# Decode attention over a 2048-key window plus a bilinear GLU: TensorE's unrolled program becomes a loop of seven turns over five heads, and four engines' programs are wrapped in a loop of two turns

## The chip, the core and the metric

The kernel runs on one core of one Trainium2 chip. The metric is the device time of one execution in microseconds (us). The kernel before takes 376.09 us, the median of three runs (375.97, 376.09 and 376.46).

## What is computed

Two tokens, one for each of the batches (B = 2), with D = 512 features, go through a layer norm, and the normalised token `xn` feeds two branches whose sum is added to the token. All data are float32.

```python
W = min(4096, max(256, Sk // 4))                  # 2048 of the 8192 cached keys
q = (xn @ wq)                                     # 32 heads of 128
scores = einsum("bhqd,bhkd->bhqk", q, k[:, :, Sk - W:]) * 128 ** -0.5
o = einsum("bhqk,bhkd->bhqd", softmax(scores), v[:, :, Sk - W:])
out = x + o @ wo + ((xn @ w_gate) * (xn @ w_up)) @ w_down    # inner width 1376
```

Every head has its own keys and values, so each of the 159.47 MB of caches and weights is used once.

## The kernel before

**The stream.** `blocks()` lists what is read, in order, as fields of some words for each of the 128 partitions: `k` and `v` (4096 words for each head, both batches side by side), `wq`, `wo`, and the weights of the GLU (`wg`, `wu`, `wr`, `wd`). The host lays the fields out in that order in one array, `stream`. SyncE's queue (SP) carries it into three slots of SBUF, `step0` to `step2`, in turn; a transfer into a slot starts when the last field that stands in it has been used (`done`, `pump`). Most transfers fill a slot with 7936 KB: the keys of one or two heads and pieces of the values of heads some three back. Behind the last full slots come shorter transfers: the last keys, the last three heads' values, and rows of `w_down`, down to 256 KB.

**One head** passes through these steps:
- `project_q`, TensorE: the token, copied over 128 columns (`xnb`), times `wq`, so that q stands in PSUM once on each partition, for both batches; four heads share a bank pair (`q0`, `q1`).
- `products`, VectorE: keys times q, in place in the slot, reading q from PSUM. `sums`, VectorE: the sum over the 128 features, which gives the scores `s` (128 x 32). `maxima`: VectorE takes each partition's largest (`m`), GpSimd the largest over partitions (`mm`).
- `weights`, ScalarE: minus the scaled maximum (`nm`), the exponentials into `p`, their sums `rs`; GpSimd sums these over partitions (`sum`), VectorE inverts (`rec`, in `reciprocals`, called behind the next head's maxima).
- `weigh`, TensorE: eight chunks of the values with `p` as stationary operand, summed in the PSUM bank `o_ps`. `copy_out`, ScalarE: the bank to `o_sb`. `transpose`, TensorE, into the bank `tr`; ScalarE scales by `rec` into `oT`. `project_o`, TensorE: `oT` times `wo`, added up in the bank `acc`.

The heads' values go through `weigh` in groups of two and one; the last heads alone.

**Order.** `Flow` records every operation as it is written in Python, finds what each depends on, and `emit` writes each engine's program in that order, one instruction behind the other with no branch. So an engine that waits holds up everything written behind it. A semaphore wait is set where an operation needs another engine or a transfer. All recorded instructions carry the line of `emit` (L243), so the profile is read by the names of the tiles.

**The end.** Behind the last keys the order is written by hand: the last heads' `pv`, `transpose` and `project_o` one by one, with matmuls into a spare bank between them (`keep_busy`) that compute nothing. The last head's values come before the last rows of `w_down`; `accumulate` spreads the final products over four partition groups of `acc`.

Of the kernel before, what the change touches and what calls it, by code (L numbers as in the profile page):

```python
# [8 lines left out]
ALU = mybir.AluOpType  # L9
# [8 lines left out]
J = W // P  # L18
# [6 lines left out]
LAG = 3  # L25
RB = 8
# [4 lines left out]
HG = 4  # L31
GC = HG * DH
JG = J // 4
CK, CQ, CO = B * J * DH, NC * GC, D
CP = CQ // NC
UNIT = CK + max(CP, CO)
STEP = 31 * FB
NP = 6
NV = CK // FB
KS = [3, 1, 2, 1, 2, 2, 1, 2, 2, 2, 1, 2, 2, 2, 1, 2, 2, 1]  # L40
WD = [(0, 2), (2, 4), (4, 7), (7, NFC - 1), (NFC - 1, NFC)]
NS = 3
BUFS = 3
BASE = 30 * 1024
FX = FR // NS

# [10 lines left out]
def blocks():  # L57

    def wd(n):
        return [("wd", i, D) for i in range(*WD[n])]

    def k(h):
        return [("k", h, CK)] + ([("wq", h, CP)] if h + HG < H else [])  # L70

    def v(h):
        return [("v", h, CK), ("wo", h, CO)]

    def gu(half):
        n = NC * (FH[half][1] - FH[half][0])
        return [("wg", half, n), ("wu", half, n)]

    ones = [("pick", 0, 8 * B), ("rows", 0, NFB * B)]
    first = [("x", 0, B * NC)] + ones + [("w", 0, NC * DH)]  # L80
    ahead = [[("w", 1, CQ - NC * DH)], gu(0) + gu(1), [("wr", 0, NS * P)] + wd(0)]
    pieces = [(h, n) for h in range(H - 1 - LAG) for n in range(NV + 1)]
    loads, h = [], 0
    for i, n in enumerate(KS):
        fields = (ahead[i] if i < len(ahead) else []) + sum((k(h + j) for j in range(n)), [])
        h += n
        room = (STEP - sum(w for _, _, w in fields)) // FB if i > 1 else 0
        taken, pieces = pieces[:room], pieces[room:]
        for g in sorted({g for g, _ in taken}):
            assert g < h - n  # L90
            ns = [m for t, m in taken if t == g]
            parts = [m for m in ns if m < NV]
            if parts:
                p0, p1 = parts[0], parts[-1] + 1
                fields.append(("vp", (g, p0, p1), FB * (p1 - p0)))
            if ns[-1] == NV:
                fields.append(("wo", g, CO))
        assert not pieces or pieces[0][0] >= h - NP
        loads.append(fields)
    assert not pieces and h == H - 1  # L100
    loads += [k(H - 1) + v(H - 1 - LAG) + wd(1)]
    out = [(("f", 0), first)] + [(("s", i), fields) for i, fields in enumerate(loads)]
    late, last = ("s", len(loads)), ("s", len(loads) + 1)
    out += [(late, v(H - 3)), (late, v(H - 2)), (last, [("v", H - 1, CK)])]
    out += [(last, [("wo", H - 1, CO)] + wd(2))]
    return out + [(last, wd(n)) for n in range(3, len(WD))]


class Flow:
# [7 lines left out]
    def __init__(self, nc):  # L117
        self.nc = nc
        self.units = {
            "pe": nc.tensor, "dve": nc.vector, "act": nc.scalar, "pl": nc.gpsimd, "sp": nc.sync,  # L120
        }
        self.ops, self.seen, self.free = [], {}, {}
        self.low = -(-nc.sbuf_base // 32) * 32
# [38 lines left out]
    def add(self, unit, make, writes, reads):  # L162
        n = len(self.ops)
        deps = set()
        for aps, write in ((reads, False), (writes, True)):
            for ap in aps:
                if not isinstance(ap.tensor, (bass.SBTensorHandle, bass.PSumTensorHandle)):
                    continue
                name, p0, p1, f0, f1 = self.box(ap)
                kept = []  # L170
                for old in self.seen.get(name, []):
                    m, w, a0, a1, b0, b1 = old
                    if m != n and (write or w) and a0 < p1 and p0 < a1 and b0 < f1 and f0 < b1:
                        deps.add((m, w))
                        if write and p0 <= a0 and a1 <= p1 and f0 <= b0 and b1 <= f1:
                            continue
                    kept.append(old)
                self.seen[name] = kept + [(n, write, p0, p1, f0, f1)]
        self.ops.append((unit, make, deps))
# [3 lines left out]

    def emit(self):
        nc, ops = self.nc, self.ops
        place, count = [], {}
        for n, (unit, make, deps) in enumerate(ops):
            key = ("dma", n) if make[0] == "dma_start" else unit
            count[key] = count.get(key, 0) + 1
            place.append((key, count[key]))  # L190
        knows = [None] * len(ops)
        known = {unit: {} for unit in self.units}
        waits = []
        for n, (unit, make, deps) in enumerate(ops):
            have = known[unit]
            need = {}
            for m, wrote in deps:
                key, at = place[m]
                if key == unit and (unit == "pe" or unit in ("dve", "act") and not wrote):
                    continue  # L200
# [7 lines left out]
            ]  # L208
            for m in keep:
# [11 lines left out]
        told = {m for keep in waits for m in keep} | {len(ops) - 1}  # L221
        sems, value, at = {}, {}, {}
        order = sorted({place[m][0] for m in told}, key=lambda key: (key in ("dve", place[-1][0]), str(key)))
        if order[-1] != place[-1][0]:
            order.append(order.pop(-2))
        for key in order:
            sems[key] = nc.alloc_semaphore("done_" + (key if isinstance(key, str) else f"load{key[1]}"))
# [7 lines left out]
        for n, (unit, (method, args, kwargs), _) in enumerate(ops):  # L235
            eng = self.units[unit]
            keep = sorted(
                waits[n], key=lambda m: (isinstance(place[m][0], tuple) and m >= landed, m)
            )
            landed = max([landed] + [m for m in keep if isinstance(place[m][0], tuple)])  # L240
# [8 lines left out]
            if n == len(ops) - 2:  # L249
                assert unit == "dve"  # L250
                nc.vector.sem_clear(range(nums[0], nums[-2]))
        assert unit == "sp"
# [19 lines left out]
def sliding_attention_plus_glu_kernel(  # L272
# [13 lines left out]
    ]  # L286


    todo, at = [], 0
    for key, fields in blocks():  # L290
        todo.append((key, fields, at))
        at += P * pitch(fields)
    tiles, used, left, got = {}, {}, {}, {}
    for key, fields, _ in todo:
        left[key] = left.get(key, 0) + len(fields)

    def pump():
        while todo:
            key, fields, at = todo[0]
            if key not in tiles:  # L300
                if key[0] == "f":
                    n = sum(w for _, _, w in fields)
                    tiles[key] = flow.tile([P, n], "first")
                elif not slots:
                    return
                else:
                    tiles[key] = slots.pop(0)
                used[key] = 0
            todo.pop(0)
            c0 = used[key]  # L310
            for kind, i, w in fields:
                got[kind, i] = (tiles[key][:, used[key] : used[key] + w], key)
                used[key] += w
            c1 = used[key]
            src = stream[at : at + P * pitch(fields)].rearrange("(p i) -> p i", p=P)
            sp.dma_start(tiles[key][:, c0:c1], src[:, : c1 - c0])

    def done(kind, i):
        _, key = got.pop((kind, i))
        left[key] -= 1  # L320
# [501 lines left out]
```

## Time and profile before

| what | value |
|---|---|
| median of the three runs | 376.09 us |
| the profiled execution's span | 374.6 us; the median is 1.5 us more, which lies around the span |
| DMA, mean | 426 GB/s, 3950 packets, 159.70 MB |
| TensorE matmul / weight load | 248.4 us (66%) / 86.8 us (23%), 1094 each |
| VectorE | 295.1 us (79%), 147 instructions |
| ScalarE | 58.1 us (16%), 259 |
| GpSimd | 25.3 us (7%), 78 |

The span runs from the first instruction to the last. "Busy" is time inside instructions; a share of the whole span mixes the stream's long middle with its start and its end, so the stages are read apart: landings of transfers from the chain of waits, durations of single operations from the timeline, the granted clock of TensorE (1.00 is full speed) from stretches of a few us. In a row of the timeline the first number is the start, the second the time, x16 the count of instructions merged into the row, and the bracket the idle time before them and what ended it. A float32 matmul of the program stands as two MATMUL records in the trace, so x16 is eight of the program's.

### The profile page before, as it was taken

The numbers are of one execution on the slowest core, as the hardware profiler recorded it, in microseconds if no ns is written. First come the engines' busy times: TensorE is split into PE (matmuls) and PEld (weight loads), VectorE is DVE, ScalarE is ACT, GpSimd is POOL, SyncE is SP. The second block draws the span as 40 slices with busy tenths as digits, with TensorE's granted clock in tenths as the row PEclk, the third lists the DMA queues.
The fourth block names the chain that finished last, engine by engine and source line by source line (L and its number), as shares of the span: only waits on it lengthen the run. The fifth ranks groups of instructions, "written<-read, shape, count | busy, mean of one in ns | idle before, by whom it ended". The sixth has DMA issues, their size and how long they took to land.

```text
span 374.6 us, 2741 instructions
## 1 busy us (share of the span) xinstructions
PE 248.4 (66%) x1094; PEld 86.8 (23%) x1094; DVE 295.1 (79%) x147; ACT 58.1 (16%) x259; POOL 25.3 (7%) x78
## 2 busy tenths in 40 slices
PE   3167675896578157855658585781488647476997
PEld 3033124231132013211212121320122112111344
DVE  3069998994599994599999945999999459999760
ACT  1002012111022012110202020300121201111232
POOL 1000000100001000000000000010001000000010
PEclk9759695898689758896969886998689868666999
DMA  8999999999999999999999999999999999999996
GB/s 345 420 465 454 450 432 435 434 434 424 427 427 434 434 434 434 436 434 441 434 435 429 434 434 434 434 429 434 434 435 434 429 434 434 428 426 416 414 432 250
DMA packets 3950, 159.70 MB, mean 426 GB/s; under 512 B 466, under 2 KB 610, under 8 KB 994
## 3 DMA queue, kind: packets, MB, share of 16 engines
q1 hardware_dynamic: 3938, 159.54, 98.6%
q8 instruction: 8, 0.13, 0.1%
q14 instruction: 4, 0.03, 0.0%
HBM read 159.47 MB, written 0.07 MB: 426 GB/s over the span
## 4 chain that ended last, share of the span: by engine, by line
DMA 64%; DVE 26%; PE 7%; ACT 1%; issue 0%; SPq 0%
DMA step<-in_stream_dram 64%; DVE s L243 13%; DVE step L243 13%; PE q L243 3%; PE acc L243 2%; PE o_ps L243 2%; PE tr L243 1%; ACT o_sb L243 0%; DVE m L243 0%; ACT oT L243 0%; DVE rec L243 0%; SPq L243 0%; DVE o_out L243 0%
## 5 line engine op out<-in xcount | busy, mean ns | idle before, releaser
L243 DVE TENSOR_TENSOR step<-step,q 128x4096 f32<-128x4096 f32 x31 | 136.8, 4411 | 47.0 <-DMA step<-in_stream_dram 47.0
L243 DVE TENSOR_REDUCE s<-step 128x32 f32<-128x4096 f32 x32 | 141.4, 4419 | 1.1
L243 PE MATMUL q<-step,xnb 128*128 128x512 f32 (+1 forms) x128 | 79.0, 759 | 80.5 <-DMA step<-in_stream_dram 80.5
L243 PE MATMUL o_ps<-step,p 128*16 128x512 f32 (+1 forms) x512 | 98.5, 730 | 11.2 <-DMA step<-in_stream_dram 11.2
L243 PEld LDWEIGHTS q<-step,xnb 128*128 128x128 f32 x128 | 28.0, 238 | 123.5 <-DMA step<-in_stream_dram 92.9
L243 PE MATMUL acc<-step,oT 128*9 128x512 f32 (+1 forms) x88 | 39.1, 604 | 8.7 <-ACT oT L243 8.7
L243 PE MATMUL tr<-first,o_sb 128*128 128x2 f32 (+2 forms) x198 | 29.1, 266 | 17.9 <-ACT o_sb L243 12.0
L243 PEld LDWEIGHTS tr<-first,o_sb 128*128 128x128 f32 x198 | 26.8, 205 | 40.6 <-ACT o_sb L243 31.3
L243 PEld LDWEIGHTS o_ps<-step,p 128*16 128x16 f32 x512 | 17.6, 107 | 78.6 <-issue 64.9
L243 ACT COPY o_sb<-o_ps 128x512 f32<-128x512 f32 (+1 forms) x24 | 13.8, 576 | 121.4 <-PE o_ps L243 121.4
L243 POOL PARTITION_ALL_REDUCE mm<-m x32 | 11.3, 355 | 268.6 <-DVE m L243 258.7
L243 ACT ACTIVATE nm<-mm 128x2 f32<-128x2 f32 x32 | 6.5, 203 | 148.0 <-POOL mm L243 148.0
L243 ACT ACTIVATE p<-s,nm 128x16 f32<-128x16 f32 x64 | 19.2, 300 | 1.0
L243 POOL PARTITION_ALL_REDUCE sum<-rs x32 | 12.7, 398 | 69.1 <-ACT p L243 69.1
L243 ACT ACTIVATE oT<-tr,rec 128x1 f32<-128x1 f32 x64 | 12.2, 260 | 27.0 <-PE tr L243 27.0
L243 DVE TENSOR_TENSOR step<-step,tr 128x4096 f32<-128x4096 f32 x1 | 4.4, 4422 | 14.8 <-DMA step<-in_stream_dram 14.8
L243 ACT ACTIVATION_READ_ACCUMULATOR p<-s,nm 128x1 f32 x64 | 11.9, 187 | 0.0
L243 PE MATMUL o_ps<-step,xn 128*2 128x512 f32 (+1 forms) x48 | 10.1, 548 | 0.0
L243 PEld LDWEIGHTS acc<-step,oT 128*9 128x9 f32 x88 | 4.6, 94 | 21.1 <-ACT oT L243 14.5
L243 DVE TENSOR_TENSOR o_out<-acc,x_nat 128x128 f32<-128x128 f32 x1 | 0.3, 292 | 8.4 <-PE acc L243 8.4
L243 DVE TENSOR_REDUCE m<-s 128x2 f32<-128x32 f32 x32 | 6.0, 186 | 1.1
L243 DVE RECIPROCAL rec<-sum 128x2 f32<-128x2 f32 x32 | 5.0, 155 | 1.9 <-POOL sum L243 1.9
(43 smaller groups left out, 41.5 us busy)
## 6 DMA issues: line engine op xcount, KB each, us to landing
step<-in_stream_dram SPq DMA_DIRECT2D x14, 7936.0 KB, 37.7
step<-in_stream_dram SPq DMA_DIRECT2D x2, 7680.0 KB, 32.0
step<-in_stream_dram SPq DMA_DIRECT2D x1, 7872.0 KB, 58.2
step<-in_stream_dram SPq DMA_DIRECT2D x1, 7808.0 KB, 38.8
step<-in_stream_dram SPq DMA_DIRECT2D x1, 4864.0 KB, 30.3
step<-in_stream_dram SPq DMA_DIRECT2D x2, 2304.0 KB, 19.6
step<-in_stream_dram SPq DMA_DIRECT2D x1, 2048.0 KB, 18.3
step<-in_stream_dram SPq DMA_DIRECT2D x1, 1024.0 KB, 19.8
```

Source lines behind the costliest of these rows:

```text
L243: made = getattr(eng, method)(*args, **kwargs)
```

## The change

**Layout.** Batch 0 lies on partitions 0 to 63 and batch 1 on 64 to 127 (`PB` = 64), for keys, values and q alike. A head still has 4096 words of keys and of values on each partition. q needs one matmul for both batches, and the maxima and the exponentials are written for each half of the partitions.

**The stream.** Three heads' keys come ahead (`AHEAD` = 3). Then six turns (`T` = 6) of three full slots of 7680 KB each bring the keys of five heads (`G` = 5), the values of the five heads three back, and the next turn's `wq`. In turn t the slot `step0` holds two heads' keys, the values of one head and five chunks of the next; `step1` holds two heads' keys, the rest of that head, a further one and one chunk; `step2` holds `wq`, one head's keys, and the rest of the values. The last turn has no fifth head of keys, and the last values and rows of `w_down` follow in eight shorter transfers. One row of `w_down` (`HOLE`) fills the gap in the last `wq`.

**TensorE's program.** The parts `q`, `a` and `b` of a turn (`part_q`, `part_a`, and `part_b` with `part_c`) read and write the same addresses in every turn, so they are written once, in a hardware loop of seven turns; the seventh does `part_a` alone. In the loop TensorE can't wait for growing semaphore values: at each waiting place it waits for a token of the engine concerned (`done_tokensp`, `done_tokenact`) and takes one away. For a transfer, SP itself waits for the landing and then gives the tokens (`tell`), in the order of its queue. `q` is in one PSUM tile of 640 columns, and ScalarE copies it to SBUF (`q_sb`, two buffers by turns, the second in the tile `first`), from where `products` reads it.

**The wrapping.** TensorE's, ScalarE's, VectorE's and GpSimd's programs each stand in a loop of two turns with `hint_back_edge`; in the first turn a branch skips all of it. SP's doesn't.

**The end.** The matmuls of `keep_busy` are gone. The last two heads' values go through one bank together; the last head is not split in two column halves any more.

```diff
+PB = P // B
+J = W // PB
+G = 5
+T = (H - 2) // G
+AHEAD = H + 1 - G * T
+SPLIT = [[0, 1], [2, 3, 4]]
+VA, VB = 5, 1
+STEP = 30 * FB
...
+        with self.nc.Fori(0, 2, engines=(eng.engine,), hint_back_edge=True) as turn:
+            with eng.If(turn > 0):
+                yield
...
+            if method == "tell":
+                m = args[0]
+                eng.wait_ge(sems[place[m][0]], value[m]).then_inc(sems["token", unit], tokens[n])
+                return
...
+                for key in sorted(points[part[0], part[2]]):
+                    eng.wait_ge(sems["token", key], 1).then_inc(sems["token", key], -1)
...
+            with nc.tensor.Fori(0, max(turns.values())) as turn:
+                for section, ns in body.items():
+                    short = turns[section] < max(turns.values())
+                    with nc.tensor.If(turn < turns[section]) if short else contextlib.nullcontext():
+                        for n in ns:
+                            write(n)
...
+    def project_q(t):
+        w = got["wq", t].rearrange("p (c n) -> p c n", c=NC)
+        for c in range(NC):
+            for n in range(0, GC, FB):
+                n1 = min(n + FB, GC)
+                pe.matmul(
+                    q_ps[:, n:n1], xnb[:, c, :], w[:, c, n:n1],
+                    start=(c == 0), stop=(c == NC - 1),
+                )
+        if t < T - 1:
+            done("wq", t)
+        act.copy(q_sb[t % 2], q_ps[:, :GC])
...
+    def scores(h, then=None):
+        products(h)
+        sums(h)
+        if then:
+            then()
+        maxima(h)
+        weights(h)
+        if h >= 1:
+            reciprocals(h - 1)
...
+    def part_a(t):
+        with flow.loop("a", t):
+            weigh(G * t, 0, NV)
+            weigh(G * t + 1, 0, VA)
+    def post(t, group):
+        d = transpose(group, copy_out(group))
+        scale_out(group, d)
+        for n in SPLIT[group]:
+            project_o(G * t + n)
+    def part_b(t):
+        with flow.loop("b", t):
+            weigh(G * t + 1, VA, NV)
+            post(t, 0)
+            weigh(G * t + 2, 0, NV)
+            weigh(G * t + 3, 0, VB)
+    def part_c(t):
+        with flow.loop("b", t):
+            weigh(G * t + 3, VB, NV)
+            weigh(G * t + 4, 0, NV)
+            post(t, 1)
+    for t in range(T):
+        part_q(t)
+        h = AHEAD + G * t
+        scores(h, lambda: part_a(t))
+        scores(h + 1)
+        scores(h + 2, lambda: part_b(t))
+        scores(h + 3)
+        if h + 4 < H:
+            scores(h + 4, lambda: part_c(t))
+        else:
+            reciprocals(h + 3)
+            part_c(t)
+    part_a(T)
+    down(HOLE)
+    acc_sb = flow.tile([M, D], "acc_sb")
+    dve.tensor_copy(acc_sb, acc)
+    weigh(H - 1, VA, NV)
+    o_sb = copy_out(0)
...
+    for c in chunks[:3]:
+        down(c)
     project_o(H - 2)
-
-    o_sb = flow.ring([P, 4 * DH], "o_sb", 2)
...
     project_o(H - 1)
-    down(3)
-    down(4)
+    for c in chunks[3:]:
+        down(c)
```

**Where instructions move.** At the end of ScalarE's program before, the exponentials of the last two heads (head 30 writes `p0`, head 31 `p1`) stand between the copies of single groups (`o_sb`); heads 25 to 28 are copied ahead of both:

```order
L243 COPY o_sb0_116<-o_ps0 128x512
L243 ACTIVATE oT1_64<-tr,rec1_111 128x1 x2
L243 ACTIVATE oT2_65<-tr,rec2_112 128x1 x2
L243 ACTIVATE oT3_66<-tr,rec3_113 128x1 x2
L243 COPY o_sb1_117<-o_ps1 128x512
L243 ACTIVATE oT0_63<-tr,rec4_114 128x1 x2
L243 ACTIVATE nm0_92<-mm0_86 128x2
L243 ACTIVATE p0_57,rs0_98<-s0_74,nm0_92 128x4x4 x2
L243 COPY o_sb0_116<-o_ps0 128x512
L243 ACTIVATE oT1_64<-tr,rec5_115 128x1 x2
L243 ACTIVATE nm1_93<-mm1_87 128x2
L243 ACTIVATE p1_58,rs1_99<-s1_75,nm1_93 128x4x4 x2
```

The end of ScalarE's program in the changed kernel (again head 30 writes `p0` and head 31 `p1`; `o_ps0` holds heads 25 and 26, and in the last row 30 and 31, `o_ps1` holds heads 27 to 29):

```order
L330 COPY o_sb0_106<-o_ps0 128x512
L330 ACTIVATE oT_62<-tr,rec_63 128x1 x4
L330 ACTIVATE nm0_94<-mm0_88 128x2
L330 ACTIVATE p0_57,rs0_69<-s0_82,nm0_94 64x8x4 x2
L330 ACTIVATE nm1_95<-mm1_89 128x2
L330 ACTIVATE p1_58,rs1_70<-s1_83,nm1_95 64x8x4 x2
L330 COPY o_sb1_107<-o_ps1 128x512
L330 ACTIVATE oT_62<-tr,rec_63 128x1 x6
L330 COPY o_sb0_106<-o_ps0 128x512
```

The copy of the group of heads 27 to 29 has moved behind the exponentials of head 31; in every turn the copy of `o_ps1` stands behind the exponentials of that turn's fourth head of keys.

On TensorE the second half of a turn (`part_c`) and the way out of the loop, in the changed kernel (the copy `o_sb1` is that of the group in `o_ps1`; the rows from `acc<-step2_51,hT_80` on stand behind the loop; what the loop's turn ends with is followed by `part_q` and `part_a` of the next turn, which in the seventh turn is `part_a` alone: eight chunks of head 30 and five of head 31):

```order
L330 MATMUL o_ps1<-step2_51,p3_60 24x512 x7
L330 MATMUL o_ps1<-step2_51,p4_61 24x512 x8
L330 MATMUL tr<-first_52,o_sb1_107 128x6 x4
L330 MATMUL acc<-step1_50,oT_62 9x512
L330 MATMUL acc<-step2_51,oT_62 9x512 x2
L357 UNCONDITIONAL_BRANCH
L354 REGISTER_ALU
L354 COMPARE_AND_BRANCH
L330 MATMUL acc<-step2_51,hT_80 9x512
L330 MATMUL o_ps0<-step1_50,p1_58 16x512 x3
L330 MATMUL acc<-acc_sb_108,carry_54 9x128 x4
L330 MATMUL tr<-first_52,o_sb0_106 128x4 x4
```

Before, matmuls of `keep_busy` stand between these steps, and heads 25 to 29 are each taken through `project_o` in rows of their own ahead of the values of head 30.

On VectorE the rows of one head before (head 26), and of one in the changed kernel (head 3):

```order
L243 TENSOR_TENSOR step0_49<-step0_49,q0 128x4096
L243 TENSOR_REDUCE s2_76<-step0_49 128x32
L243 TENSOR_REDUCE m2_82<-s2_76 128x2
L243 RECIPROCAL rec1_111<-sum1_105 128x2
L243 TENSOR_TENSOR step0_49<-step0_49,q0 128x4096
```

```order
L330 TENSOR_TENSOR step0_49<-step0_49,q_sb_79 128x4096
L330 TENSOR_REDUCE s3_85<-step0_49 128x32
L330 TENSOR_REDUCE m3_67<-s3_85 64x1 x2
L330 RECIPROCAL rec_63<-sum2_102 128x2
L330 TENSOR_TENSOR step0_49<-step0_49,q_sb_79 128x4096
```

The product's second operand lies in SBUF (`q_sb`) where it lay in PSUM (`q0`), and the maxima are two instructions where they were one.

More of the change, by code (lines that the diff above doesn't have):

```diff
@@ L100, in blocks, with k, vp @@
[L100 to L106, printed above, removed]
+    def k(*heads):
+        return [("k", h, CK) for h in heads]
+    def vp(h, p0=0, p1=NV):
+        return [("vp", (h, p0, p1), FB * (p1 - p0))] + ([("wo", h, CO)] if p1 == NV else [])
```

621 lines of the change are left out of this document (301 added, 320 removed).

## The prediction

> **What bounds the kernel now.** I read the page first, then the chain of waits, then the timeline of the last 20 us.
>
> ```profile
> span 374.6 us, 2741 instructions
> q1 hardware_dynamic: 3938, 159.54, 98.6%
> q8 instruction: 8, 0.13, 0.1%
> DMA 64%; DVE 26%; PE 7%; ACT 1%; issue 0%; SPq 0%
> ```
>
> The 16 DMA engines carry data in 98.6% of the span: the stream is the bound, and the engines' shares in the chain are work that lies beside transfers already under way. Two landings from the chain of waits give the rate:
>
> ```profile
> 58.02 39.69 DMA step<-in_stream_dram
> ...
> 284.36 38.13 DMA step<-in_stream_dram
> ```
>
> The first lands at 97.71, the second at 322.49, and twelve transfers of 7936 KB lie between: 18.73 us each, 423.7 KB/us. At the end (timeline, then stretches of 1 us with PE, PEld, DVE, ACT, POOL, clock, DMA share and GB/s):
>
> ```profile
> 372.26 0.12 PEld L243 LDWEIGHTS acc<-step,hT 128*9 128x9 f32 x8 [0.22 <-DMA step<-in_stream_dram]
> 372.74 0.29 DVE L243 TENSOR_TENSOR o_out<-acc,x_nat 128x128 f32<-128x128 f32 x1 [8.38 <-PE acc L243]
> ```
>
> ```profile
> 370.00:371.00 1.00, 1.00 (x16) 0.94 (x19) 0.00 (x0) 0.30 (x2) 0.00 (x0) 1.00 0.69 264
> 371.00:372.00 1.00, 1.00 (x44) 0.96 (x40) 0.00 (x0) 0.36 (x2) 0.00 (x0) 1.00 0.31 121
> ```
>
> The last piece lands at 372.2, and 2.4 us later the span ends. So today the compute work behind the last landing is tiny: it has been fitted to the stream. The share of 0.69 and 0.31 shows that the DMA engines stop raggedly, the first at about 370.3.
>
> **Part 1: the stream keeps its bytes.** 311,462 words on each of 128 partitions are read by either kernel (159.47 MB), so while the queue never drains the stream takes as long as now. The first 7951 KB are there when VectorE starts:
>
> ```profile
> 21.98 4.42 DVE L243 TENSOR_TENSOR step<-step,tr 128x4096 f32<-128x4096 f32 x1 [14.81 <-DMA step<-in_stream_dram]
> ```
>
> 7951 / 423.7 = 18.8, so the stream begins at 3.2. Changed kernel: the slots of turn 0 land at 55.4, 73.5 and 91.6 (22,099 KB, then 7680 KB or 18.13 us each, 54.4 a turn), the last turn's `step0` at 327.4 and `step1`, with the keys of heads 30 and 31, at 345.5; 10,752 KB follow, and the stream ends at 370.9. The 1.3 us against today's 372.2 are within the raggedness; I keep 370.3 and 372.2 as ends. Fewer instruction packets (8 of 16 KB on q8, for TensorE's unrolled program) can't gain more than that.
>
> The Trainium skill (Runtime: NRT & Kernel Launch, Instruction fetch mechanics) gives TensorE's instruction memory as 128 KiB and also says that only two 16 KiB lines are held. By the first the 641 instructions I count in TensorE's program would stay resident and q8 would fall silent, at best 370.3; by the second the loop, of some 265, would be fetched anew in every turn. The eight packets now, one for each 256 or so of 2188 instructions, go with the second.
>
> **Part 2: the start can drain the queue once.** Turn 0's q stands on TensorE behind the whole GLU:
>
> ```profile
> 44.13 10.05 PE L243 MATMUL o_ps<-step,xn 128*2 128x512 f32 x48
> 58.64 0.60 PE L243 MATMUL tr<-first,o_sb 128*128 128x6 f32 x2 [4.45 <-DVE o_sb L243]
> 63.72 0.60 PE L243 MATMUL tr<-first,o_sb 128*128 128x6 f32 x2 [0.24 <-ACT hX L243]
> ```
>
> `step2` lands at 37.2, the matmuls end at 47.3, the gate's copy waits for the exponentials of head 2 (three heads of 9.2 us on VectorE from 19.6, see below, and 1.7) until 48.8, copy and gate's product (1.3 together) take it to 50.1, the seven transposes (58.64 to 64.3) to 55.8, the first rows of `w_down` 4 us (2.8 warm to 5.5 cold, 12 records at the rates below) to 59.8. q of five heads is eight records of 512 columns and eight of 128:
>
> ```profile
> 97.75 3.78 PE L243 MATMUL q<-step,xnb 128*128 128x512 f32 x4 [6.53 <-DMA step<-in_stream_dram]
> 113.61 1.98 PE L243 MATMUL q<-step,xnb 128*128 128x512 f32 x4
> ```
>
> That is 5.0 warm, 9.4 cold; I take 6.5, and 0.75 for the copy of 640 columns (below, 0.71 for 512 with its semaphores): VectorE begins head 3 at 67.0, 11.6 behind its landing. `step0` is free only when `wo` of the turn's first head has been used, behind two heads on VectorE (18.4), their exponentials (1.7) and copy, transposes, scaling and one projection (4.9): 92.0, and some 1 us to the first bytes, against 91.6 when the queue drains. Price 1.4 us (0 if all is warm, 5.8 if all is cold). From turn 1 on the same release comes some 10 us ahead of need.
>
> **Part 3: in the turns the work hides.** One head on VectorE, and its largest to its exponentials:
>
> ```profile
> 331.60 4.40 DVE L243 TENSOR_TENSOR step<-step,q 128x4096 f32<-128x4096 f32 x1
> 336.04 4.42 DVE L243 TENSOR_REDUCE s<-step 128x32 f32<-128x4096 f32 x1
> 340.49 0.19 DVE L243 TENSOR_REDUCE m<-s 128x2 f32<-128x32 f32 x1
> 340.60 0.15 DVE L243 RECIPROCAL rec<-sum 128x2 f32<-128x2 f32 x1
> 340.67 4.40 DVE L243 TENSOR_TENSOR step<-step,q 128x4096 f32<-128x4096 f32 x1
> ...
> 361.44 0.19 DVE L243 TENSOR_REDUCE m<-s 128x2 f32<-128x32 f32 x1
> ```
>
> ```profile
> 362.89 0.19 ACT L243 ACTIVATION_READ_ACCUMULATOR p<-s,nm 128x1 f32 x1
> ```
>
> 9.07 us a head, 9.17 with the second maximum; 1.64 from the maximum to the exponentials, 1.74 now. That q comes from SBUF instead of PSUM no large product here shows; two small ones do, the first with both operands in SBUF:
>
> ```profile
> L243 DVE TENSOR_TENSOR sq<-xc 128x8 f32<-128x8 f32 x1 | 0.2, 168 | 0.0
> L243 DVE TENSOR_TENSOR xc<-first,tr 128x8 f32<-128x8 f32 x1 | 0.2, 163 | 0.7 <-PE tr L243 0.7
> ```
>
> 168 against 163 ns: I cost it at nothing, and no gain is to be had from it, since the sum, which reads one operand, takes the same 4.42. (A product of twice the time would make a head 13.6 and a turn 68 us; nothing here points to it.) Five heads are 45.9 of a turn's 54.4. TensorE's rates, with the granted clock in the last but two columns:
>
> ```profile
> 322.54 3.61 PE L243 MATMUL o_ps<-step,p 128*16 128x512 f32 x16 [5.74 <-DMA step<-in_stream_dram]
> 326.85 1.87 PE L243 MATMUL tr<-first,o_sb 128*128 128x4 f32 x8 [0.71 <-ACT o_sb L243]
> 329.23 2.73 PE L243 MATMUL acc<-step,oT 128*9 128x512 f32 x3 [0.50 <-ACT oT L243]
> ...
> 340.61 6.37 PE L243 MATMUL o_ps<-step,p 128*16 128x512 f32 x38 [5.31 <-DMA step<-in_stream_dram]
> 348.47 1.05 PE L243 MATMUL tr<-first,o_sb 128*128 128x4 f32 x8
> 349.45 2.74 PE L243 MATMUL acc<-step,oT 128*9 128x512 f32 x6
> 352.75 1.91 PE L243 MATMUL o_ps<-step,p 128*16 128x512 f32 x16
> 354.48 1.88 PE L243 MATMUL acc<-step,hT 128*9 128x512 f32 x4
> ```
>
> ```profile
> 323.00:327.00 4.00, 3.29 (x17) 0.49 (x9) 3.97 (x2) 0.96 (x4) 0.40 (x1) 0.50 0.92 399
> 349.00:352.00 3.00, 3.00 (x11) 0.89 (x10) 0.78 (x3) 0.72 (x4) 0.35 (x1) 1.00 0.80 345
> ```
>
> Cold (clock 0.50) a value record costs 0.226 us, warm 0.119, and the burst of 38 from cold pays 1.85 over its warm time. `part_c` and `part_q` from the landing of `step2`: 30 value records 5.4, copy 0.7, transposes 1.5, scaling 0.5, three projections 2.7, q 5.0, 0.9 for half a cold burst, copy 0.75: 17.4 of the 18.1 us before the next keys land. Just hidden; all cold, VectorE starts a turn some 2 us late.
>
> **Part 4: the end is no longer hidden.** This decides. The last turn's `step0` lands at 327.4 + 1.4 = 328.8; four heads on VectorE run from there without a gap (36.4 to the maximum of head 31), and its exponentials end 1.74 later, at 367.0. Today they end at 363.1. Behind them, by ScalarE's order, comes the copy of the group of heads 27 to 29, whose values have been summed since about 361, and all of TensorE's remaining program waits for that copy. Small records:
>
> ```profile
> 367.31 0.41 PE L243 MATMUL acc<-step,oT 128*9 128x128 f32 x8
> ...
> 371.71 0.95 PE L243 MATMUL acc<-step,hT 128*9 128x128 f32 x24
> ```
>
> The chain from 367.0: copy with its semaphores 0.71 (the idle time before the transposes, above); eight transposes, cold after the wait, 1.87; scaling 0.50 (that before `acc`); six projection records 2.74; eight chunks of head 30 and five of head 31, 26 records, 3.1; the row in the gap 0.94; three more chunks 0.71; one cold burst 1.85; copy 0.71; transposes 1.05; three rows of `w_down` 0.95; two projections 0.82; four rows 1.27. Sum 17.2, so 384.2. Then 1.9 as now (372.7 to 374.6): span 386.1. The median stands 1.5 above the profiled span (376.09 against 374.6): **387.6 us**, 11.5 more than now. All warm and without the drain (14.5 from 364.9) it is 382.8; with the drain, the late turn and the stream at their upper ends 395. A fifth of a per cent, 0.75 us, is about what a measurement here can tell from no change.
>
> **Rivals.**
> Not slower: the work behind the last keys stays under the stream, which then ends at 370.3 to 370.9, and with today's 2.4 the time is 374.2 to 374.8. It decides only if the chain behind head 31 takes under 4 us where rows give 14.5 warm; I see no way round ScalarE's order. 5 in 100.
>
> The loop's branches fetch code. The eight packets take 0.1% of 16 engines' span, 0.75 us each; with the way there and back a stall of perhaps 1.5 to 3 us (estimate) at each turn's branch. That eats the 0.8 us of cover of part 3 and delays the last turn by 2.2, and it falls into the end chain once: +5.2, 392.8 (389 to 398). Nothing in this trace shows a branch. It is also the way in which the change doesn't do what it says. 18 in 100.
>
> GpSimd waits for VectorE's product:
>
> ```profile
> 331.70 0.35 POOL L243 PARTITION_ALL_REDUCE mm<-m  x1 [7.84 <-DVE m L243]
> ```
>
> Now the reduction runs inside the next product, which began 0.10 earlier and reads q from PSUM. If a product with two SBUF operands kept GpSimd out, the reduction would come 4.3 us later for every head with a product behind it. The fourth head's exponentials gate the copy of `o_ps1` and so the next q: 36.4 + 1.74 + 4.3 + 13.4 (copy to q in SBUF, cold) = 55.9 us a turn, over the stream's 54.4. Five turns from 67.0: 346.5, then 38.1, 17.2, 1.9 and 1.5: 405 (397 if warm). The Trainium skill (SBUF — State Buffer, SBUF: two separate sides) states such a lock for a VectorE operation with two SBUF inputs against a GpSimd operation that reads SBUF, the first to start holding it. Against it: now a second maximum on another half of the partitions stands there, and GpSimd may come first by a hair. 30 in 100.
>
> **The numbers.** My forecast has 47 in 100. Its own range is 382.8 to 395, the other slower cases reach to 405 and somewhat over; 382 to 408 leaves out the case that isn't slower and the tail of the lock. Faster 0.03, same 0.02, slower 0.95.
>
> **What would show it.** Right: head 31's exponentials end near 367, ScalarE's copy of `o_ps1` starts right behind them, TensorE idles some 5 us before it, and the last piece of the stream has landed ten us before `o_out`. Part 2: a dip of the DMA near 92. Fetch: gaps of PE after each turn's last `acc`, more packets on q8. Lock: GpSimd's `mm` starting as a product ends. Wrong: `o_out` within 3 us of the last landing.

## The result, and the profile after

The changed kernel takes **410.28 us** (median of four runs, 410.06 to 410.56) against 376.05 us before: ratio 1.0907, 95% interval 1.0892 to 1.0923. That is 34.2 us more, where 11.5 were forecast; it lies 2.3 us above the range's upper end and close to the rival in which GpSimd waits for VectorE's product (405). The profiled execution took 410.19, with a span of 408.8.

From the page of the changed kernel, the span, what the DMA engines moved in each fortieth of it, the two queues that were shown of before, and the costliest group of instructions:

```profile
span 408.8 us, 2646 instructions
...
GB/s 361 430 463 410 451 422 445 427 349 192 385 463 397 475 391 391 385 445 409 457 379 415 379 463 403 463 367 427 379 463 403 397 385 451 409 396 245 253 388 8
...
q1 hardware_dynamic: 4226, 159.54, 92.4%
q8 instruction: 2, 0.03, 0.0%
...
L330 POOL PARTITION_ALL_REDUCE mm<-m x32 | 109.9, 3435 | 224.9 <-DVE m L330 224.9
```

The bytes are the same, but the stream fills only 92.4% of the span (98.6% before). The last row is the new one: GpSimd's 32 reductions to the largest take 3435 ns on average; in the row of before that the prediction shows, one took 0.35 us. The timeline of the end of turn 1 (start, duration, engine, what, and in brackets the idle time of the engine and what ended it) tells which:

```profile
162.13 4.64 POOL L330 PARTITION_ALL_REDUCE mm<-m  x1 [3.15 <-DVE m L330]
162.15 4.41 DVE L330 TENSOR_TENSOR step<-step,first 128x4096 f32<-128x4096 f32 x1
166.59 4.42 DVE L330 TENSOR_REDUCE s<-step 128x32 f32<-128x4096 f32 x1
166.81 0.20 ACT L330 ACTIVATE nm<-mm 128x2 f32<-128x2 f32 x1 [8.31 <-POOL mm L330]
...
167.69 0.18 ACT L330 ACTIVATION_READ_ACCUMULATOR p<-s,nm 64x1 f32 x1
167.90 0.58 ACT L330 COPY o_sb<-o_ps 128x512 f32<-128x512 f32 x1
...
168.63 1.84 PE L330 MATMUL tr<-first,o_sb 128*128 128x6 f32 x8 [7.09 <-PEq L322]
...
171.07 4.02 PE L330 MATMUL acc<-step,oT 128*9 128x512 f32 x6 [0.59 <-PEq L322]
...
171.51 0.35 POOL L330 PARTITION_ALL_REDUCE mm<-m  x1 [3.15 <-DVE m L330]
...
175.02 4.59 PE L330 MATMUL q<-step,xnb 128*128 128x512 f32 x16
179.65 0.69 ACT L330 COPY q_sb<-q 128x640 f32<-128x640 f32 x1 [6.68 <-PE q L330]
...
180.44 4.43 DVE L330 TENSOR_TENSOR step<-step,q_sb 128x4096 f32<-128x4096 f32 x1 [8.82 <-ACT q_sb L330]
```

The reduction that begins together with a product ends 0.21 us behind that product's end (166.56) and takes 4.64; the turn's fifth, behind which VectorE stands still, takes 0.35. From the late maximum the rest of the turn is one chain: exponentials, copy of the group, transposes, projections, the next q, its copy, and only then VectorE's next product. VectorE idles 8.82 us there. It begins its six turns at 67.5, 124.6, 180.4, 237.4, 294.8 and 350.9, 56.7 us apart on average, while the stream would need 54.4. At the end:

```profile
388.40 0.35 POOL L330 PARTITION_ALL_REDUCE mm<-m  x1 [3.15 <-DVE m L330]
...
389.67 0.18 ACT L330 ACTIVATION_READ_ACCUMULATOR p<-s,nm 64x1 f32 x1
389.88 0.58 ACT L330 COPY o_sb<-o_ps 128x512 f32<-128x512 f32 x1
...
390.61 1.03 PE L330 MATMUL tr<-first,o_sb 128*128 128x6 f32 x8 [2.04 <-PEq L322]
...
405.21 0.29 DVE L330 TENSOR_TENSOR o_out<-acc,x_nat 128x128 f32<-128x128 f32 x1 [1.95 <-PE acc L330]
405.53 0.35 SPq L330 DMA_DIRECT2D out_dram<-o_out  x1
```

Head 31's exponentials end at 389.9, the copy of the group of heads 27 to 29 starts right behind them, and 15.3 us later the last addition begins. The stream ended at 398.8.

### The profile page after: what moved, and what is told of

Read it like the earlier page. It is cut to its first block, busy times and chain, and to the rows that moved or that the text cites. A ratio compares the mean times of both kernels' runs of the same rounds, so it can differ in the third digit from the quotient of the medians.

```text
span 408.8 us, 2646 instructions
## 1 busy us (share of the span) xinstructions
PE 199.8 (49%) x940; PEld 72.8 (18%) x940; DVE 302.4 (74%) x179; ACT 59.5 (15%) x250; POOL 124.3 (30%) x84
## 3 DMA queue, kind: packets, MB, share of 16 engines
q1 hardware_dynamic: 4226, 159.54, 92.4%
## 5 line engine op out<-in xcount | busy, mean ns | idle before, releaser
L330 POOL PARTITION_ALL_REDUCE mm<-m x32 | 109.9, 3435 | 224.9 <-DVE m L330 224.9
L330 PE MATMUL o_ps<-step,p 128*24 128x512 f32 (+1 forms) x512 | 81.6, 666 | 64.2 <-PEq L322 64.2
L330 DVE TENSOR_TENSOR step<-step,q_sb 128x4096 f32<-128x4096 f32 x15 | 66.1, 4409 | 34.8 <-ACT q_sb L330 34.8
L330 DVE TENSOR_TENSOR step<-step,first 128x4096 f32<-128x4096 f32 x14 | 61.7, 4409 | 29.0 <-ACT first L330 29.0
L330 PE MATMUL tr<-first,o_sb 128*128 128x6 f32 (+1 forms) x118 | 25.7, 336 | 101.2 <-PEq L322 98.9
L330 PEld LDWEIGHTS o_ps<-step,p 128*24 128x24 f32 (+1 forms) x512 | 18.4, 103 | 111.6 <-issue 110.2
L330 PE MATMUL q<-step,xnb 128*128 128x512 f32 (+1 forms) x96 | 27.9, 444 | 0.0
L330 ACT ACTIVATE p<-s,nm 64x32 f32<-64x32 f32 x64 | 20.4, 319 | 1.4
L330 PEld LDWEIGHTS q<-step,xnb 128*128 128x128 f32 x96 | 15.1, 193 | 18.4 <-issue 18.4
L330 DVE TENSOR_REDUCE m<-s 64x1 f32<-64x32 f32 x64 | 11.5, 180 | 1.5
L330 ACT ACTIVATION_READ_ACCUMULATOR p<-s,nm 64x1 f32 x64 | 11.8, 185 | 0.0
```

Of the source, the lines that this page charges most:

```text
L330: made = getattr(eng, method)(*args, **kwargs)
```

## The experiments

The theory is the lock: a product with both operands in SBUF keeps GpSimd's reduction waiting until it ends, and that lengthens each turn. The rivals are the loop with its branches, tokens and empty first turns, and the order of the work (start and end) without any lock. Unless another base is named, the edit is one to the changed kernel. Each ratio is to the kernel before (375.98 to 376.18 in the four series).

**e3: the kernel before with q in SBUF.** ScalarE copies each head's q from PSUM to SBUF, one head ahead; nothing else of the kernel before is altered but a ring of the scores, 4 in place of 6 for lack of room.

```diff
-        qb = q_ps[g][:, :, hh * DH : (hh + 1) * DH] if h else q_first
+        qb = q_in.pop(h) if h else q_first
...
+            q_in[h + 1] = flow.ring([P, B, DH], "qs", 2)
+            act.copy(q_in[h + 1], q_ps[g][:, :, hh * DH : (hh + 1) * DH])
```

> The kernel before, with nothing changed but that ScalarE copies each head's q to SBUF one head ahead and the product reads it there (and a ring of score tiles is four deep instead of six, for room). Theory of the lock: the mm reductions take 4.6 us wherever a product stands ready behind the maximum, 0.35 where VectorE waits for keys; since values lag the keys by three heads here, the time stays within 1 per cent: 376 to 379. Rival B (halves): reductions stay at 0.35. Rival A says nothing of this run.

376.30 us, ratio 1.0006 (0.9997 to 1.0016). Its timeline, a head with a product behind it, and head 30, behind which VectorE waits for the next keys:

```profile
331.62 4.40 DVE L243 TENSOR_TENSOR step<-step,qs 128x4096 f32<-128x4096 f32 x1
331.73 4.51 POOL L243 PARTITION_ALL_REDUCE mm<-m  x1 [4.51 <-DVE m L243]
...
349.87 0.35 POOL L243 PARTITION_ALL_REDUCE mm<-m  x1 [3.10 <-DVE m L243]
```

With q in PSUM the reduction at this place took 0.35; with q in SBUF it takes 4.51 and ends 0.22 behind the product. So the lock is there without loop, tokens or new layout. And here it costs no time: the values wait for their landing anyway. The delay itself is not the price; what stands behind it is.

**e1: the changed kernel with q in PSUM**, in one buffer instead of two by turns.

```diff
-    q_sb = [flow.tile([P, GC], "q_sb"), first[:, sum(w for _, _, w in blocks()[0][2]) - NC * FIRST :][:, :GC]]
+    q_sb = [flow.bank([P, 4 * FB // 2], "q_cp")[:, :GC]] * 2
```

> The changed kernel, but ScalarE copies q to another PSUM tile instead of SBUF, so that VectorE's products have one SBUF operand. Theory (a product with two SBUF operands keeps GpSimd's reduction over partitions out until it ends, and the fourth head's exponentials, late by that, hold back the copy of the values' group and so the next turn's q): the mm reductions fall from 4.64 to 0.35 us, a turn from 57.1 to the stream's 54.4, and the time comes to the sum of the prediction's own case, 387.6 (383 to 393). Rival A (the turn is long because of the loop's branches, tokens and a cold TensorE; the long reductions are hidden): reductions short, turns still 57, time 408 to 411. Rival B (the reduction is slow because its input is now written in two halves of the partitions): reductions stay at 4.64, time 410.

393.84 us (392.21 to 395.22), ratio 1.0483 (1.0463 to 1.0503): 16.4 us of the 34.2 go with this one line. From its page, and its timeline at head 31 and the end:

```profile
L330 POOL PARTITION_ALL_REDUCE mm<-m x32 | 11.3, 354 | 305.6 <-DVE m L330 305.6
```

```profile
361.16 0.35 POOL L330 PARTITION_ALL_REDUCE mm<-m  x1 [7.43 <-DVE m L330]
361.18 4.40 DVE L330 TENSOR_TENSOR step<-step,q_cp 128x4096 f32<-128x4096 f32 x1
...
372.01 0.59 ACT L330 COPY o_sb<-o_ps 128x512 f32<-128x512 f32 x1
...
387.84 0.29 DVE L330 TENSOR_TENSOR o_out<-acc,x_nat 128x128 f32<-128x128 f32 x1 [1.95 <-PE acc L330]
```

The product is as long as before (4.40), the reduction beside it short. VectorE's turns begin at 67.2, 120.2, 172.3, 223.7, 278.5 and 333.0: 51.3 to 53.0 us apart while they make up for the start, 54.5 to 54.8 from then on, close to the stream's 54.4. This is the kernel that the forecast described; it came 0.84 above the range expected of it, and what it missed is taken apart below.

**e2: the next product behind the reduction.** VectorE scales the maximum itself, so that its next product can't begin before GpSimd is done.

```diff
-        nm = flow.ring([P, B], "nm", 6)
-        act.mul(nm, mm, -SCALE)
+        nm = flow.ring([P, B], "nm", 6)
+        dve.tensor_scalar(nm, mm, -SCALE, None, op0=ALU.mult)
```

> The changed kernel with q in SBUF as it is, but VectorE instead of ScalarE scales the reduced maximum, ahead of the next product, so that the product can't start before the reduction has ended. Theory of the lock: reductions 0.35, a head on VectorE 9.4 + 0.7 = 10.1 us, five heads 50.5 of a turn's 54.4, time 386 to 393. Rival A (loop): 408 or more. Rival B (the halves): reductions stay at 4.64 and now stand on VectorE's path, a turn 71 us, time near 490.

402.91 us, ratio 1.0703 (1.0684 to 1.0722): 7.4 us are won, not 17 to 24. GpSimd in its timeline:

```profile
98.34 0.36 POOL L330 PARTITION_ALL_REDUCE mm<-m  x1 [4.70 <-DVE m L330]
99.86 3.69 POOL L330 PARTITION_ALL_REDUCE sum<-rs  x1 [1.17 <-ACT p L330]
108.24 0.36 POOL L330 PARTITION_ALL_REDUCE mm<-m  x1 [4.70 <-DVE m L330]
```

The maxima are free (0.36), but the exponentials now come while the product runs (98.88 to 103.29), so their sum falls into it and waits in place of the maximum (3.69; 0.40 in the changed kernel, where the sum comes behind the product). And a head takes 9.90 us, 0.5 more than the 9.38 of the changed kernel, for the round trip over GpSimd. The turns are 54.2 to 54.6 us, hardly shorter than the stream's share, so the lag of the start is never made up. The expectation left out both.

**e8: the product in two instructions** of 16 keys each, q in SBUF as in the changed kernel.

```diff
-        dve.tensor_tensor(
-            kt, kt, q.unsqueeze(1).to_broadcast([P, J, DH]), op=ALU.mult
-        )
+        for j in range(0, J, J // 2):
+            kj = kt[:, j : j + J // 2, :]
+            dve.tensor_tensor(
+                kj, kj, q.unsqueeze(1).to_broadcast([P, J // 2, DH]), op=ALU.mult
+            )
```

> The changed kernel with q in SBUF as it is, but every product as two instructions of 16 keys each (2.2 us) in place of one of 32. If what keeps GpSimd out is held for one VectorE instruction, the reduction runs between the two halves: mm about 2.4 us in place of 4.64, a turn 53.6 in place of 55.8, and the time lies between the changed kernel's and that with q in PSUM: 398 to 403. If GpSimd stays out for as long as VectorE's instructions follow one another without a gap, mm stays at 4.6 and the time at 410 to 412 (two more instructions' start a head, some 0.06 us each).

399.97 us, ratio 1.0637 (1.0610 to 1.0663), in the range of the first theory. In its timeline:

```profile
105.01 2.51 POOL L330 PARTITION_ALL_REDUCE mm<-m  x1 [4.70 <-DVE m L330]
105.03 4.47 DVE L330 TENSOR_TENSOR step<-step,q_sb 128x2048 f32<-128x2048 f32 x2
...
108.71 1.05 POOL L330 PARTITION_ALL_REDUCE sum<-rs  x1 [1.19 <-ACT p L330]
```

The maximum comes through between the halves, at 107.5; the sum, ready in the middle of the second half, waits for its end. GpSimd is kept out for one VectorE instruction, not for the train of them.

**e4: the last group ahead of head 31.** On the base of e1; in the last turn the group of heads 27 to 29 is recorded before the maxima and exponentials of head 31.

```diff
-        scores(h + 3)
         if h + 4 < H:
+            scores(h + 3)
             scores(h + 4, lambda: part_c(t))
         else:
+            scores(h + 3, lambda: part_c(t))
             reciprocals(h + 3)
-            part_c(t)
```

> As e1 (q in PSUM), and in the last turn the copy and scaling of the group of heads 27 to 29 stand ahead of the exponentials of head 31 in ScalarE's program instead of behind them. If the prediction's part 4 holds (all of TensorE's rest waits for that copy), the copy, the transposes, three projections and head 30's values, some 8 us, leave the chain behind head 31's exponentials: e1 less 6 to 9 us, 378 to 382. If the end is set by something else, e1's time.

385.60 us, ratio 1.0244 (1.0223 to 1.0264): 8.2 less than e1, as wide a step as expected; the time lies above the 378 to 382 that were worked out from the forecast's 387.6 for e1. The copy (timeline) now comes 4.2 us ahead of head 31's maximum instead of behind its exponentials:

```profile
367.33 0.59 ACT L330 COPY o_sb<-o_ps 128x512 f32<-128x512 f32 x1 [3.75 <-PE o_ps L330]
...
371.50 0.36 POOL L330 PARTITION_ALL_REDUCE mm<-m  x1 [7.43 <-DVE m L330]
```

**e7: turn 0's q ahead of the GLU.** On the base of e4. TensorE's looped instructions have to stand in one piece, so the loop's turn is rotated: the q of the next turn ends it.

```diff
+    project_q(0)
     for half in range(2):
         project_gu(half)
...
-        part_q(t)
...
-            scores(h + 4, lambda: part_c(t))
+            scores(h + 4, lambda: (part_c(t), part_q(t + 1)))
```

> The kernel of e4 with the projection of turn 0's q ahead of the GLU on TensorE (the loop's turn is rotated: q of the next turn ends it). Theory: the drain at the start comes from q standing behind the GLU (VectorE begins head 3 at 67.0 in e4, 11 us behind its keys), and it moves everything behind it by 4 to 5 us, since the turns are nearly as long as their share of the stream. Then VectorE begins head 3 at about 56, the second turn's first slot lands at 109 to 110 in place of 113.4, the stream ends near 372, head 31's product starts near 357, and the time is 380 to 381.5. Rival: the turns of 52 to 54.5 us are bound by their own chain, the lag grows again, and no more than 1 to 2 us are won: 383.5 to 385.

379.81 us, ratio 1.0118 (1.0089 to 1.0146): 5.8 less than e4, a little more than the theory gave. From its page, and the start of turn 1 in its timeline:

```profile
span 377.4 us, 2652 instructions
...
q1 hardware_dynamic: 4226, 159.54, 98.0%
```

```profile
110.86 4.42 DVE L330 TENSOR_TENSOR step<-step,q_cp 128x4096 f32<-128x4096 f32 x1 [7.33 <-DMA step<-in_stream_dram]
```

The stream is the bound again: every full slot lands 18.1 us behind the one before, and VectorE's turn begins when its slot lands, not when q does.

**e5, e6, e9, e11: what the loops cost.** e5 is e4 without the wrapping, e6 is e4 without wrapping and with TensorE's program unrolled; e11 and e9 are the same two on the base of e7.

```diff
-TWICE = ("pe", "act", "dve", "pl")
+TWICE = ()
```

For e6 and e9, beside this, the parts are not marked as looped, so TensorE's program is written out as the other engines' are.

```diff
-        self.part = (section, t)
-        self.count.setdefault(self.part, 0)
...
-                if unit == "pe":
+                if False:
                     write_looped(ns)
```

> The kernel of e4 (q in PSUM, the last turn's group ahead of the last head's maxima; 385.6 us) without the loop of two turns around the four engines' programs; TensorE's loop of seven turns stays. If an empty turn costs only the 5.8 us at the start by which VectorE's first operations come later (6.67 us against 0.82 in the trace of before), and these lie under the landing of the first keys at about 20 us, the time stays within 1 us of e4: 384.6 to 386.6. If branches cost something that the trace doesn't show (instructions fetched behind each of them), 1.5 to 4 us are won: 381.5 to 384.

> The kernel of e4 with no loop at all: TensorE's program written out turn by turn and no wrapping, with the order of every instruction the same. If the loop itself costs nothing (a wait through a token 0.6 us late, hidden), 384.6 to 386.6, with eight packets on q8 in place of one. If the tokens or branches sit on the turns' chain, the turns get shorter by the 0.3 to 0.6 us of each token on it, and the time falls by 2 to 4 us: 381.5 to 383.5.

> The kernel of e7 (379.8 us; its stream no longer drains) with no loop at all: TensorE unrolled, nothing wrapped. e5 and e6 changed little on a base that waits for its own chain in each turn; here the stream sets the turns, and only the two ends can move. In the wrapped kernels the first keys land at 20.7, in the others at 19.7; if that is the empty turn's doing, the whole stream comes 1.0 earlier: 378.2 to 379.2. If the loop also costs at the end (its last branch, tokens in the last turn), 377 to 378. If nothing, 379.4 to 380.2.

> The kernel of e7 without the wrapping, TensorE's loop of seven turns kept. Beside e7 and the unrolled one of this call it tells the empty turn from the loop. If the first keys land at 19.7 and this sets the end, 378.2 to 379.2, as the unrolled kernel; if the wrapping costs nothing, 379.4 to 380.2.

| | wrapped and looped | looped only | neither |
|---|---|---|---|
| base e4 | 385.60 (384.69 to 387.40) | e5 385.37 (383.67 to 386.04) | e6 383.67 (383.20 to 384.71) |
| ratio | 1.0244 (1.0223 to 1.0264) | 1.0230 (1.0210 to 1.0251) | 1.0195 (1.0180 to 1.0210) |
| base e7 | 379.81 (379.54 to 382.53) | e11 380.82 (379.01 to 382.58) | e9 379.74 (378.39 to 380.21) |
| ratio | 1.0118 (1.0089 to 1.0146) | 1.0118 (1.0099 to 1.0137) | 1.0093 (1.0078 to 1.0107) |

e5 and e9 came out as expected if the loops cost nothing; e6 lies between its two ranges and e11 0.6 above both of its. The wrapping costs nothing that shows, though the first keys land 1.0 us earlier without it (19.7 against 20.7), from which I had expected a gain. Unrolling TensorE gives 1.1 to 1.7 us against the looped kernel without wrapping, with intervals that touch or overlap. Both loops together cost 1.9 us on the base of e4 (385.60 against 383.67, intervals apart) and 0.1 on that of e7. So they cost at most some 2 us of 34; whether they cost anything where the stream sets the turns stays open.

**e10: e7 with q back in SBUF** (the edit of e1 undone).

> The kernel of e7 with q back in SBUF, so that GpSimd's maximum waits for VectorE's product again, and everything else stays. Theory: the lock costs what a turn has over the stream's share. A turn's chain with the lock is 37.4 (four heads on VectorE) + 5.8 (to the fourth head's exponentials) + 12.5 (copy to q) = 55.7, the stream's share 54.35: five turns, 6.9 us, and the time is 386 to 388. Rival: the lock costs what it cost between the changed kernel and e1 (16.4 us), wherever the stream stands: 395 to 397. In between (391) if the turns take 56.7, the mean of the changed kernel's.

395.54 us, ratio 1.0515 (1.0499 to 1.0530): 15.7 more than e7, where the theory gave 7 and the rival 16.4. Of the theory's price two parts were missing. Turn 0 takes 55.8 as worked out (56.6 to 112.5), but the five together 283.3 us against the stream's 271.7 (VectorE's turns in e7), 11.7 more and not 6.9. And in the last turn (timeline):

```profile
358.74 4.64 POOL L330 PARTITION_ALL_REDUCE mm<-m  x1 [3.15 <-DVE m L330]
...
364.51 0.58 ACT L330 COPY o_sb<-o_ps 128x512 f32<-128x512 f32 x1
...
367.82 2.72 PE L330 MATMUL acc<-step,oT 128*9 128x512 f32 x3 [0.60 <-PEq L322]
...
369.72 4.66 SPq L330 DMA_DIRECT2D step<-in_stream_dram  x6
```

Head 29's late maximum holds the copy of `o_ps0`, that the projections, and these the slot into which SP's next six transfers go: they are issued 16.1 us later than in e7 (353.63), 11.8 of it from the turns and 4.3 from this. So the rival's number is met by a sum that it didn't name: the turns' excess, and one lock on the way to the last transfers.

**e12: e10 with the product in four instructions** (as e8, with `J // 4`).

> The kernel of e10 (395.5 us: q of the next turn ends a turn, q in SBUF) with every product in four instructions of eight keys. e8 gave 2.51 us for the maximum with two instructions (a half of 2.2 and its own 0.35), so four should give 1.4. Theory (the lock lasts for one instruction, and costs what a turn's chain has over the stream's share of 54.35): the chain is 55.8 - 3.2 = 52.6, plus at most 0.2 us a head for three more instructions, so the stream sets the turns again, the second turn's first slot lands at 110.9 and the last turn's at 328.2 as in e7, and the end bears one late maximum of 1.1 us: 380.5 to 382, with no PSUM spent on q. Rival: the reductions, sums too now, wait for several quarters in a row, since VectorE's next instruction takes hold again before GpSimd does: mm 2.5 to 4.6 and 386 to 395.

383.21 us (381.60 to 384.42), ratio 1.0182 (1.0160 to 1.0204), 12.3 less than e10. In its timeline:

```profile
66.00 1.44 POOL L330 PARTITION_ALL_REDUCE mm<-m  x1 [14.81 <-DVE m L330]
66.02 4.61 DVE L330 TENSOR_TENSOR step<-step,q_sb 128x1024 f32<-128x1024 f32 x4
...
68.63 1.12 POOL L330 PARTITION_ALL_REDUCE sum<-rs  x1 [1.19 <-ACT p L330]
```

The maximum takes 1.44 as worked out, the four products 4.61 instead of 4.41, and the turns' first slots land at 110.7 to 328.0, as in e7: in the turns the lock is paid off. The end is 1.2 us above the range. The last transfers are issued 1.3 us later than in e7 (354.95 against 353.63) but land no later (372.75 against 372.94); what comes late in the profiled execution is TensorE. Its `o_ps` records ahead of the copy of heads 27 to 29 end 2.4 us later (364.15 against 361.78), and its last 72 records, at a granted clock of 0.50 from 376 to 378 where e7's ran at 1.00, take 3.8 us for 2.2.

## Why the prediction was wrong

The sign, the mechanism of the end and VectorE's start at 67 held. The number failed at one sentence of part 3; the rival that named this failure came within 5.3 us of the time, with some errors that cancel.

**The step that failed: "That q comes from SBUF … I cost it at nothing".** On VectorE that is so: the product takes 4.40 to 4.43 us from either memory. The cost lay on another engine. The rows that I set against each other (168 and 163 ns) were two small VectorE operations with no GpSimd work beside them; they could not show what the operand does to a neighbour. The reduction inside the product, 0.35 with q in PSUM, takes 4.64, and e1 puts 16.4 us on it. The Trainium skill (SBUF — State Buffer, SBUF: two separate sides) has this rule, and I gave it 30 in 100. e3 and e1 agree with it for the product's second operand. What I held against it, that GpSimd may come first by a hair, doesn't help: the reduction's record begins 0.02 us ahead of the product's and still ends 0.21 behind it. For the same reason the sign that I named, `mm` starting as a product ends, isn't what the trace shows: `mm` starts with the product and lasts until its end.

**The rival's size: 405, measured 410.19.** VectorE began at 67.5 for 67.0. A turn of 55.9 is met only in turn 1 (55.8), where TensorE's clock comes up earliest, and by other parts: four heads 37.5 for 36.4, 5.8 for 6.0 to the exponentials, copy to q 12.5 for 13.4. The other four take 56.1 to 57.4: the six `acc` records of turn 0 take 5.24 us and those of turn 2 5.11 (granted clock 0.51 and 0.53), against 4.02 in turn 1 above (0.66). The last turn so begins 4.4 late, its exponentials end 38.95 behind it for 38.1, the chain is 15.3 for 17.2, and 3.6 us for 1.9 lie between the last addition and the span's end: 405 + 4.4 + 0.85 - 1.9 + 1.7 = 410.05. What the turns have over the stream also rests on a cold TensorE: at a clock of 1.00 eight transposes take 1.03 us (390.61 above; 1.84 in turn 1) and six `acc` records took 2.74 before, so a warm TensorE would shorten the chain by some 2 to 3 us a turn (estimate from these rows), about the whole excess. No run tried that, and none brought the matmuls of `keep_busy` back.

**My own case without the lock is e1**, 392.2 in its profiled run against 387.6. The last `step0` lands at 332.6 and not 328.8: the slots land 1.0 later from turn 0 on (56.4, 74.5, 92.6), and the drain of part 2 costs 4.2 (113.4 and 133.0, 2.6 and 1.6 over a pace of 18.1), inside its bounds of 0 to 5.8 but not the 1.4 that I took. Then 0.4 to the first product, 1.0 for heads of 9.38 us (the second maximum was to add 0.10 to a head's 9.07 and added 0.31), 0.2 less to the exponentials, 1.4 less for the chain, 1.2 more for the output: 387.6 + 3.8 + 0.4 + 1.0 - 0.2 - 1.4 + 1.2 - 0.2 (the time around the span) = 392.2.

**Part 1** held for the pace (18.1 a slot) and for the end of an undrained stream within 2 us (372.9 in e7, 370.9 forecast). q8 fell nearly silent, 2 packets for 8 before, and the loop is not fetched again in each turn. This is what the Trainium skill's 128 KiB for TensorE's instruction memory gives (Runtime: NRT & Kernel Launch, Instruction fetch mechanics). It doesn't rule out its two lines, to which I had assigned the eight packets of before: at some 256 instructions to a packet of 16 KB the loop's 265 could stand in two lines as well, so that no fetch in each turn had to follow from them.

**Part 2** named the place, and e7 shows it: with q ahead of the GLU the drain is gone, worth 5.8 us. In the changed kernel it is larger still. Its windows of 3 us (last two columns the DMA's busy share and GB/s):

```profile
91.00:94.00 3.00, 1.04 (x5) 1.07 (x6) 3.00 (x1) 1.59 (x6) 0.40 (x1) 0.50 0.00 0
94.00:97.00 3.00, 2.40 (x6) 0.97 (x7) 2.92 (x5) 0.72 (x4) 1.31 (x1) 0.50 0.00 0
```

The queue stands empty for these 6 us, since the release of `step0` waits for the second head's exponentials, and these for a locked maximum. That the same release comes 10 us ahead of need from turn 1 on is roughly right for e1 (5.5 to 11.0 us before the transfer ahead of it lands) and wrong for the changed kernel (2.3 to 3.1), whose later slots come up to 21 us apart.

**Part 4** was right in its mechanism (the copy starts 0.03 us behind head 31's exponentials) and in size: e4 takes it away for 8.2 us.

**The fetch rival** (18 in 100) is out: at most some 2 us by e4 to e7, e9 and e11, and in the changed kernel no packet in any turn (its two start at 4.1 and 406.2).

Undone one after the other, the lock gives 16.4 us, the group at the end 8.2, q behind the GLU 5.8, the loops 0.1; 3.7 remain of 34.2. By the traces of e7 and before, 0.7 of them is the stream's end (372.9 against 372.2) and 2.1 the work behind it, whose last addition starts at 375.5 against 372.7; the rest lies around the span, where e7's profiled execution has 2.5 us and the one before 1.5. No run undid these. No version here beats the kernel before.

## What to carry to other kernels

An operand's home is a cost for the engines beside it: before moving one operand of a long VectorE operation from PSUM to SBUF, look for every GpSimd operation that runs beside it and follow what waits for that. The delay costs what the chain behind it has over the stream's share (nothing in e3; 11.7 us over five turns of e10, and 4.3 more at its end); cutting the long operation into quarters won back most of it for 0.2 us a head. An order by turns, as this one, gathers such a chain: what was a delay of one head becomes the turn's length.

## What the runs showed of the hardware

- A reduction over partitions on GpSimd ends 0.2 to 0.3 us behind the VectorE product with two SBUF operands beside which it starts: 4.64 us for one of 4.41, 2.51 for halves, 1.44 for quarters (behind the first of them), 0.35 alone or beside a product that reads q from PSUM. VectorE's sum over the features, with one operand, doesn't hold it: the `sum` reductions that run beside it take 0.40.
- VectorE's first instruction starts at 6.67 us in the changed kernel, where its program stands in a loop of two turns with an empty first one, and at 0.82 in e5, without; the wait for the first keys hides it.
- The output transfer takes 1.5 to 1.6 us from issue to landing in the kernel before and in nine of the runs. In four it takes longer: 3.3 us in the changed kernel, 3.2 in e12, 2.7 in e1 and 2.6 in e8. In these four, and in no other, an instruction packet of 16 KB on q8 starts while it is under way (in the changed kernel at 406.2, between 405.53 and 408.81); e5 and e11 show two packets as well, both earlier, and 1.5. That the packet stands in its way is argued, not tried.
